# Retention into a bilinear feed-forward on one core: loads and DMA transposes of the last six chunks in another order, two products and a difference moved to GpSimd

## The chip, the cores and the metric

The kernel runs on one core of one Trainium2 chip. The metric is the device time of one execution in microseconds, as the median over the runs of the same program; lower is better. Inside the core, TensorE (PE), VectorE (DVE), ScalarE (ACT), GpSimd (POOL) and SyncE (SP) each work through a list of instructions of their own in a fixed order, and wait for each other through semaphores. In this kernel SP computes nothing: it issues nearly all of the DMAs.

## What is computed

A linear recurrence with one decay rate per head (retention), whose output is the input of a bilinear feed-forward:

```python
def _attn_ref(q, k, v):                       # 4 batches, 8 heads, 768 positions, 64 wide, float32
    gamma = 1.0 - 2.0 ** (-5.0 - np.arange(H))
    scale = 1.0 / np.sqrt(D)
    for t in range(S):
        state = gamma[None, :, None, None] * state + np.einsum('bhd,bhe->bhde', k[:, :, t], v[:, :, t])
        y[:, :, t] = scale * np.einsum('bhd,bhde->bhe', q[:, :, t], state)

x = y.transpose(0, 2, 1, 3).reshape(3072, 512)
out = ((x @ w_a) * (x @ w_b)) @ w_out         # 512 -> 1536 -> 512
```

## The kernel before

**Slots.** The 4 x 768 positions are cut into 24 slots of 128. For a slot the kernel loads k, q and v from HBM (`load_slot`, L117 to L129; q for two slots at once, L138), multiplies k and q with tables of powers of gamma and writes them as bf16 into one tile `kqb` (`scaled`, L281 to L292, two instructions on POOL), casts v to bf16 (`vb`, L251 on POOL, or L249 on ACT for slots 12 to 19), and turns `kqb` into `kqT` with a DMA transpose that SP issues (`flip`, L326 to L329). `casts(t)` (L299) does this for slot t, and between the steps it puts the loads of slot t + 2 on SP's queue.

**PE on a pair of slots.** `turn(new, old)` (L419) takes two slots. For the new pair it updates the running state from `kqb` and `vb` (`update`, matmuls of L375) and computes the scores from `kqT` (`scores`, matmuls of L357, the higher slot of the pair first). For the old pair it computes y (L395 and L405). ACT brings y to SBUF as `xt`, the feed-forward's x.

**Feed-forward.** The slots are joined to blocks (`TILES`, L16): block 4 is slots 10 and 11, block 5 is slots 12 to 15, and the last block is slots 16 to 23. The attention runs ahead of the feed-forward: while PE works on block 5, slots 18 to 23 are loaded, scaled, transposed and scored. Per tile of 128 features a block computes a = x w_a (L553) and g = x w_b (L565); ACT brings a to SBUF (L556), and DVE multiplies it with g from PSUM into h (`ht`, L567). Twelve such tiles make h, and h w_out follows.

**Strassen-Winograd.** The larger products are done with seven block products where eight would be usual, so they need sums of blocks beforehand. `hsum` (L627) makes the sums of h (`hs`), `xf_sum` and `x_sum` those of x, `weight_pieces` those of the weights (`wea`, `web`, `wsa`, `wsb`). In block 5 the class `Quad` (L913) does four of the feature tiles this way: `a` and `b` are its two weights for one pair of tiles, `c` and `d` for the next, and `p1` to `p7` are the seven products (`b5` is product 5 of `b`). Its method `leave` (L954) forms g as product plus snapshot on DVE and then multiplies it with the half of a (`asb`) on DVE or POOL: h = h * asb, SBUF operands only, 128x256 each, all of it at L603, the line of the helper `tt`.

**What sets the order.** All of it is written by hand. The helper `seq` makes each instruction depend on the one before it on the same engine, so that the order of the calls is the order on every engine. The part that the change touches is the string `LACED` (L26), which interleaves the second product of block 4 (`m`) with the Quads of block 5 and with calls such as `S20` (casts of slot 20) or `F2` and `G2` (a and g of feature tile 2), and the calls after it (L1192 to L1207): slots 18 and 19 before the string, 20 and 21 in it, 22 and 23 behind it. SP's queue is one list too: a transpose that stands behind a load is issued after it.

**Names in the rows.** `kf`, `qf`, `vf` are the loaded k, q, v; `kqb` is scaled k and q in natural layout, `kqT` the transposed pair; `ht` is h, `hs1` to `hs4` its sums; `fa`, `fb`, `mA` to `mC`, `uA` to `uC` are PSUM banks of the block products.

Of the kernel before, what the change touches and what calls it, by code (L numbers as in the profile page):

```python
# [12 lines left out]
ALU = mybir.AluOpType  # L13
# [9 lines left out]
       "S02 S01 b7 a2 b2 S04 a6 b6 S13 a5 b5 S12 a3 b3 a4 b4 S11 c7 d7 c6 d6 S14 c5 d5 "  # L23
       "c3 c4 d4 d3")
V_LATE = range(12, 20)
LACED = ("X3 X2 m1 m7 m2 a1 b1 a2 b2 m6 X1 a6 b6 a7 b7 F2 X4 m5 a5 b5 S20 G2 a3 b3 a4 b4 V18 S21 "  # L26
         "m3 c1 d1 F3 H3 c2 d2 c6 d6 c7 d7 c5 d5 m4 c3 d3 V19 c4 d4 G3")
LOADS = "p0 p1 w0 w1 a1 b1 a2 k2 q2 b2 v2 o0 o1 o2 o3 o4 o5 s6 t8".split()

# [2 lines left out]
def kernel(  # L32
# [10 lines left out]
    nc = tc.nc  # L43
    P = 128
    B, H, S, D = q.shape
# [6 lines left out]
    NSLOT = B * NCH  # L52
# [59 lines left out]
    def raw_tile(shape, dtype, tag, name):  # L112
        return raw.tile(shape, dtype, tag=tag, name=name, bufs=3 if tag == "vf" else 2)

    raws, wst, whole = {}, {}, {}

    def load_slot(t, names="kqv"):  # L117
        b, ci = divmod(t, NCH)
        for nm in names:
            src = {"k": k, "q": q, "v": v}[nm]  # L120
            if nm == "q":
                if t % 2 == 0:
                    load_two(nm, src, b, ci // 2, t)
                continue
            if t % 2 == 0:
                whole[nm] = raw_tile([P, 2, H, D], F32, nm + "f", nm + "f")
            raws[nm, t] = whole[nm][:, t % 2]
            s = src[b, :, ci * P : (ci + 1) * P, :].rearrange("h p d -> p h d")
            seq(nc.sync.dma_start(out=raws[nm, t], in_=s))  # L129
# [5 lines left out]
    def load_two(nm, src, b, u, t):  # L135
        f = raw_tile([P, H, 2, D], F32, nm + "f", nm + "f")
        s = src[b, :, 2 * u * P : 2 * (u + 1) * P, :].rearrange("h (p two) d -> p h two d", two=2)
        seq(nc.sync.dma_start(out=f, in_=s))  # L138
        for par in range(2):
            raws[nm, t + par] = f[:, :, par, :]  # L140
# [106 lines left out]
    def cast(engine, dst, src):  # L247
        if engine is nc.scalar:
            seq(nc.scalar.copy(dst, src))  # L249
        else:  # L250
            seq(engine.tensor_copy(dst, src))  # L251
# [19 lines left out]
    kb, qb, vb, kqT, aT = {}, {}, {}, {}, {}  # L271
# [9 lines left out]
    def scaled(eng, t, i):  # L281
        tab = tabs[0] if i else tabs[1 if t < 2 * PAIRS else 2]
        dst, src, tab = kqb[t][:, i], raws["kq"[i], t], tab[:, t % NCH]
        if t < 2 * PAIRS:
            dst, src = (x.rearrange("p (hp r) d -> p hp r d", r=2) if x is src else x
                        for x in (dst, src))
            tab = tab.rearrange("p (hp r) o -> p hp r o", r=2).to_broadcast([P, HP, 2, D])
        else:
            dst = dst.rearrange("p hp r d -> p r hp d")
            src = src.rearrange("p (r hp) d -> p r hp d", r=2)  # L290
            tab = tab.rearrange("p (r hp) o -> p r hp o", r=2).to_broadcast([P, 2, HP, D])
        seq(eng.tensor_tensor(dst, src, tab, op=ALU.mult))  # L292

    def new_nat(t):
        kqb[t] = nat.tile([P, 2, HP, 2, D], BF16, tag="kqb", name="kqb")
        kb[t], qb[t] = kqb[t][:, 0], kqb[t][:, 1]
        vb[t] = nat.tile([P, H, D], BF16, tag="vb", name="vb")

    def casts(t, between=lambda: None):  # L299
        new_nat(t)  # L300
        scaled(nc.gpsimd, t, 0)
        between()
        scaled(nc.gpsimd, t, 1)
        if t not in range(12, 20):
            cast(nc.gpsimd, vb[t], raws["v", t])
        u = t + 2
        if u in (20, 22):
            load_slot(u, "kq")
            load_slot(u + 1, "k")
        flip(t)  # L310
        if u in V_LATE:
            if u == 13:
                load_slot(12, "q")
            elif u == 19:
                load_slot(18, "kq")
            load_slot(u, {12: "k", 18: ""}.get(u, "kq"))
            if u % 2:
                load_slot(u - 1, "v")
                load_slot(u, "v")
        elif u in (20, 22):  # L320
            load_slot(u, "v")
            load_slot(u + 1, "v")
        elif u < 20:
            load_slot(u)

    def flip(t):  # L326
        if t % 2 == 0:
            kqT[t // 2] = tra.tile([P, 2, 2, HP, P], BF16, tag="kqT", name="kqT", bufs=3)
        seq(nc.sync.dma_start_transpose(  # L329
            out=kqT[t // 2][:, t % 2].rearrange("p a b c -> p (a b) c"),  # L330
            in_=kqb[t].rearrange("p a hp r d -> p (a hp r d)")))

    def casts_two(t):
        for u in (t, t + 1):
# [267 lines left out]
    def tt(dst, x, y, op, eng=nc.vector):  # L602
        seq(eng.tensor_tensor(dst, x, y, op=op))  # L603
# [23 lines left out]
    def hsum(J, s, a, b, eng=nc.vector):  # L627
        U = slice(int(J == 0), 2 if isinstance(J, tuple) else TILES[J] // 2)
        hs_tile(J, s)
        v = ht[J].rearrange("p (k j) (u r n) -> p r k j u n", k=2, r=2, n=P)  # L630
        A11, A12, A21, A22 = (v[:, r, k2, a:b, U] for r in range(2) for k2 in range(2))
        S = {x: hs[J, x][:, a:b, U] for x in (1, 2, 3, 4) if (J, x) in hs}
        x, y, op = {3: (A11, A21, ALU.subtract), 2: (A22, S[3], ALU.subtract), 1: (A21, A22, ALU.add),
                    4: (A12, S.get(2), ALU.subtract)}[s]
        tt(S[s], x, y, op, eng)
# [116 lines left out]
    def laced(order):  # L752
        made = {"m": Group(4, 0, Y0, AT0, Y1)}
        for p in range(2):
            made.update({"ac"[p]: Quad(p, "a", AT1, "kqT2"), "bd"[p]: Quad(p, "b", Y1, "aT")})
        ht[5] = htp.tile([P, NFT, 4 * P], BF16, tag="ht", name="ht")
        for x in order.split():
            if x[0] == "H":
                hsum(5, int(x[1]), 0, 1)
            elif x[0] in "XFGVS":  # L760
                {"X": xf_sum, "F": lambda f: (store(), ffn_a(5, f)), "G": lambda f: ffn_g(5, f), "V": v_cast,
                 "S": casts}[x[0]](int(x[1:]))
            else:
                getattr(made[x[0]], "p" + x[1])()

# [147 lines left out]
    class Quad:  # L913
# [40 lines left out]
        def leave(self, i, c, bank, n):  # L954
            cols = slice(c * DH, (c + 1) * DH)
            if self.w == "a":
                tt(self.half(i)[:, cols], self.bank[bank], self.snaps[n], ALU.add)
                return
            h = ht[5][:, NP * i + self.p, cols]
            tt(h, self.bank[bank], self.snaps[n], ALU.add)  # L960
            tt(h, h, self.half(i)[:, cols], ALU.mult, nc.gpsimd if (i, c) == (1, 0) else nc.vector)

        def p1(self):
            self.A = self.whole(FF)
# [64 lines left out]
    D_, G_, A_ = nc.vector, nc.gpsimd, nc.scalar  # L1029
    K, Q = 0, 1  # L1030
# [167 lines left out]
    hsums(4, 3, 6, G_)  # L1198
    casts(19)
    laced(LACED)  # L1200
    casts(22)
    turn(18, 16)
    hsum(5, 3, 1, 2)
    hsum(5, 2, 0, 2, G_)
    casts(23)
    blocks(5, 4, 6)
    blocks(5, 8, 9)  # L1207
    weight_pieces(2)
# [37 lines left out]
```

## Time and profile before

| | us |
|---|---|
| runs shown | 219.98, 220.09, 223.73 |
| median | 220.09 |
| the profiled execution: its time | 220.76 |
| its span in the profile | 219.0 |
| PE busy | 210.7 (96% of the span) |
| POOL busy | 153.5 (70%) |
| DVE busy | 149.8 (68%) |
| ACT busy | 102.9 (47%) |
| granted TensorE clock, mean | 0.998 |

The time of the profiled execution is 1.76 us more than its span, since the span begins at the first instruction and ends at the last. A busy PE means that its matmuls follow one another; their ends are modelled. The page's DMA share is that of the mean of 16 DMA engines and goes above 1 where transfers overlap in the records. Rows of the timeline give the start, the duration, the engine, the line and the tiles, and in brackets how long the engine stood idle just before and who ended it.

### The profile page before, as it was taken

The page shows a single profiled execution, that of the slowest core. Times are in us where ns is not written, and L with a number is a line of the kernel's source. Part 1 is how long each engine was busy: PE and PEld are TensorE (multiplying, and loading weights), DVE is VectorE, ACT ScalarE, POOL GpSimd, SP SyncE. Part 2 cuts the span into 40 slices and gives each one's busy share as a digit, 9 for nine tenths or more (in the row PEclk, how much of TensorE's full clock was granted, in tenths as well). Part 3 has the DMA queues.
Part 4 walks back from the last instruction along what each step waited for, and adds up shares of the span by engine and source line. Part 5 has one row for each costly group of instructions (what it writes and reads, how often), then busy time and mean ns, then how long its engine had stood idle before and what let it go on. Part 6 is the DMA issues. An engine that isn't in the chain of part 4 may idle for free.

```text
span 219.0 us, 5716 instructions
## 1 busy us (share of the span) xinstructions
PE 210.7 (96%) x2252; PEld 146.0 (67%) x2252; DVE 149.8 (68%) x276; ACT 102.9 (47%) x231; POOL 153.5 (70%) x184
## 2 busy tenths in 40 slices
PE   7889999999999999999999999799999999999994
PEld 3557445687458888888888776356874444448883
DVE  3777346846984494464478989477576987788962
ACT  3256325342234435464566566344546566652331
POOL 5266876778778759989679968599996999540000
PEclk9999999999999999999999999999999999999999
DMA  6999999999999999999998999950013000000055
GB/s 167 290 322 367 385 308 359 381 253 234 200 257 239 203 230 221 188 221 264 166 229 208 217 189 217 221 122 3 3 48 145 0 0 3 1 0 0 27 192 168
DMA packets 85162, 39.68 MB, mean 181 GB/s; under 512 B 57488, under 2 KB 78864, under 8 KB 85136
## 3 DMA queue, kind: packets, MB, share of 16 engines
q1 hardware_dynamic: 84992, 39.26, 77.3%
q8 instruction: 17, 0.28, 0.5%
q14 instruction: 9, 0.07, 0.1%
q10 hardware_dynamic: 144, 0.07, 0.1%
HBM read 28.31 MB, written 6.29 MB: 158 GB/s over the span
## 4 chain that ended last, share of the span: by engine, by line
PE 82%; DMA 6%; DVE 4%; SPq 3%; POOL 1%; issue 1%; DVEq 0%
PE a L553 16%; PE g L565 16%; PE mA L670 11%; PE uA L844 9%; PE mB L670 6%; PE o L590 5%; PE uB L844 5%; SPq L138 3%; DMA wsta<-in_moe_w_a_dram 3%; PE mC L670 3%; DMA kqT<-kqb 3%; PE uC L844 2%; PE at L357 2%; PE y L405 2%; DVE ht L603 1%; PE st L375 1%
## 5 line engine op out<-in xcount | busy, mean ns | idle before, releaser
L567 DVE TENSOR_TENSOR ht<-g,asb 128x256 bf16<-128x256 f32 (+1 forms) x70 | 34.4, 492 | 30.8 <-PE g L565 27.8
L553 PE MATMUL a<-xt,wa_bf 128*128 128x256 bf16 (+1 forms) x280 | 48.6, 300 | 0.1
L565 PE MATMUL g<-xt,wb_bf 128*128 128x256 bf16 (+1 forms) x280 | 48.4, 300 | 0.0
L556 ACT CAST asb<-a 128x256 bf16<-128x256 f32 (+1 forms) x70 | 30.0, 428 | 34.6 <-PE a L553 32.9
L565 PEld LDWEIGHTS <-wb_bf 128*128 128x128 bf16 x280 | 27.0, 98 | 10.2
L553 PEld LDWEIGHTS <-wa_bf 128*128 128x128 bf16 x280 | 26.5, 98 | 10.7 <-POOL wa_bf L251 0.4
L292 POOL TENSOR_TENSOR kqb<-kf,ktab 128x512 bf16<-128x512 f32 x22 | 23.3, 1064 | 6.8 <-DMA kf<-in_k_dram 4.6
L851 ACT COPY snap<-uA 128x512 f32<-128x512 f32 x36 | 20.0, 587 | 15.4 <-PE uA L844 13.9
L670 PEld LDWEIGHTS <-hs 128*128 128x128 bf16 x234 | 22.8, 98 | 3.6
L363 DVE TENSOR_TENSOR aT<-at,mask 128x512 bf16<-128x512 f32 x36 | 22.3, 681 | 1.9 <-PE at L357 1.7
L292 POOL TENSOR_TENSOR kqb<-qf,qtab 128x512 bf16<-128x512 f32 x18 | 19.3, 1070 | 4.0 <-DMA qf<-in_q_dram 4.0
L603 POOL TENSOR_TENSOR ht<-gsb,asb 128x512 bf16<-128x512 bf16 x13 | 15.2, 1174 | 7.2 <-DVE gsb L603 7.1
L677 ACT COPY snaps<-mA 128x256 f32<-128x256 f32 x30 | 11.0, 374 | 19.0 <-PE mA L670 18.9
L670 PEld LDWEIGHTS <-ht 128*128 128x128 bf16 x180 | 17.5, 98 | 3.3
L251 POOL CAST vb<-vf 128x512 bf16<-128x512 f32 x16 | 9.9, 635 | 11.4 <-DMA vf<-in_v_dram 9.5
L603 POOL TENSOR_TENSOR hs<-ht 128x384 bf16<-128x384 bf16 (+2 forms) x13 | 15.2, 1167 | 3.0 <-DVE ht L567 3.0
L603 POOL TENSOR_TENSOR hs<-ht,hs 128x384 bf16<-128x384 bf16 (+1 forms) x17 | 16.8, 993 | 0.6 <-DVE ht L567 0.5
L670 PE MATMUL mA<-wsum,hs 128*128 128x256 bf16 x120 | 15.2, 273 | 0.0
L603 DVE TENSOR_TENSOR osb<-mB,snaps 128x256 f32<-128x256 f32 x20 | 8.4, 421 | 8.6 <-ACT snaps L677 4.7
L590 PE MATMUL o<-wo_bf,ht 128*128 128x512 bf16 x48 | 10.7, 379 | 0.0
L249 ACT CAST gst<-st 128x256 bf16<-128x256 f32 x14 | 5.2, 372 | 11.3 <-PE st L375 11.3
L603 DVE TENSOR_TENSOR gsb<-uB,snap 128x512 bf16<-128x512 f32 x12 | 8.2, 686 | 2.9 <-ACT snap L851 2.1
(138 smaller groups left out, 375.9 us busy)
## 6 DMA issues: line engine op xcount, KB each, us to landing
qf<-in_q_dram SPq DMA_DIRECT2D x12, 512.0 KB, 6.1
out_dram<-osb SPq DMA_DIRECT2D x21, 256.0 KB, 4.0
kf<-in_k_dram SPq DMA_DIRECT2D x18, 256.0 KB, 5.4
vf<-in_v_dram SPq DMA_DIRECT2D x18, 256.0 KB, 5.3
wsta<-in_moe_w_a_dram SPq DMA_DIRECT2D x6, 512.0 KB, 7.7
wsto<-in_moe_w_out_dram SPq DMA_DIRECT2D x6, 512.0 KB, 8.7
wstb<-in_moe_w_b_dram SPq DMA_DIRECT2D x5, 512.0 KB, 8.2
kf<-in_k_dram SPq DMA_DIRECT2D x3, 512.0 KB, 7.2
```

The lines of the kernel that those rows point to most:

```text
L292: seq(eng.tensor_tensor(dst, src, tab, op=ALU.mult))
L363: seq(nc.vector.tensor_tensor(aT[t][:, r], at[r], mask.to_broadcast([P, HP, P]), op=ALU.mult))
L553: seq(nc.tensor.matmul(a, wa_bf[:, kt, fs], xcols(J, kt, c0, c1), start=(kt == 0), stop=(kt == KT - 1)))
L556: seq(nc.scalar.copy(asb, a))
L565: seq(nc.tensor.matmul(g, wb_bf[:, kt, fs], xcols(J, kt, c0, c1), start=(kt == 0), stop=(kt == KT - 1)))
L567: seq(nc.vector.tensor_tensor(ht[J][:, ft, c0:c1], g, asbs.pop((J, ft, c0)), op=ALU.mult))
L590: seq(nc.tensor.matmul(o, ht[J][:, ft, i * P : (i + 1) * P], wo_bf[:, ft], start=(ft == 0), stop=(ft == NFT - 1), skip_group_check=True))
L603: seq(eng.tensor_tensor(dst, x, y, op=op))
L670: seq(nc.tensor.matmul(m, w, right[:, j], start=(first and j == 0), stop=(j == NP - 1), skip_group_check=True))
L677: seq(nc.scalar.copy(self.snaps[:, n], self.bank["A"]))
L844: seq(nc.tensor.matmul(m, w, right[:, k], start=(first and k == 0), stop=(k == 1), skip_group_check=True))
L851: seq(nc.scalar.copy(self.snaps[n], self.bank["A"]))
```

## The change

The change rewrites the order around slots 18 to 23:

- `casts(18)` no longer puts all loads of slots 20 and 21 between its scaling and its transpose. SP now issues the k and q loads of slot 20, the transpose of 18, the k load of 21; then, with `casts(19)`, the transpose of 19, both v loads, and the k and q loads of slot 22.
- Slots 20 and 21 are scaled together (`late_kq`, as K20), all four scalings and both transposes one behind the other; the k load of 23 and the v loads of 22 and 23 come behind the transposes. The casts of v of both slots follow as `late_v` (L20), later in the string. Slots 22 and 23 are done in the same manner behind the string, ahead of and behind `turn(18, 16)`.
- In `Quad.leave` POOL makes all products h * asb with i = 1, where before it made one of two. In block 5 that moves two products (b5 and d5) from DVE to POOL; a 128x256 difference, `hsum(5, 3, 1, 2)`, moves as well. Two differences of h stand ahead of the scaling of slots 22 and 23.

```diff
-LACED = ("X3 X2 m1 m7 m2 a1 b1 a2 b2 m6 X1 a6 b6 a7 b7 F2 X4 m5 a5 b5 S20 G2 a3 b3 a4 b4 V18 S21 "
+LACED = ("X3 X2 m1 m7 m2 a1 b1 a2 b2 m6 X1 a6 b6 a7 b7 F2 X4 m5 a5 b5 K20 G2 a3 b3 a4 b4 V18 L20 "
          "m3 c1 d1 F3 H3 c2 d2 c6 d6 c7 d7 c5 d5 m4 c3 d3 V19 c4 d4 G3")
...
 def casts(t, between=lambda: None):
...
         u = t + 2
-        if u in (20, 22):
+        if u == 20:
             load_slot(u, "kq")
+        flip(t)
+        if u == 20:
             load_slot(u + 1, "k")
-        flip(t)
+            return
+        if u == 21:
+            load_slot(u - 1, "v")
+            load_slot(u, "v")
+            load_slot(22, "kq")
+            return
...
-        elif u in (20, 22):
-            load_slot(u, "v")
-            load_slot(u + 1, "v")
...
+    def late_kq(t):
+        for u in (t, t + 1):
+            new_nat(u)
+            scaled(nc.gpsimd, u, 0)
+            scaled(nc.gpsimd, u, 1)
+            flip(u)
+        if t == 20:
+            load_slot(23, "k")
+            load_slot(22, "v")
+            load_slot(23, "v")
+
+    def late_v(t):
+        for u in (t, t + 1):
+            cast(nc.gpsimd, vb[u], raws["v", u])
...
-            tt(h, h, self.half(i)[:, cols], ALU.mult, nc.gpsimd if (i, c) == (1, 0) else nc.vector)
+            tt(h, h, self.half(i)[:, cols], ALU.mult, nc.vector if i == 0 else nc.gpsimd)
...
     laced(LACED)
-    casts(22)
+    hsum(5, 3, 1, 2, G_)
+    hsum(5, 2, 0, 2, G_)
+    late_kq(22)
     turn(18, 16)
-    hsum(5, 3, 1, 2)
-    hsum(5, 2, 0, 2, G_)
-    casts(23)
+    late_v(22)
```

**SP, from the first load of slot 20 to the transpose of slot 21.** `kqb_2288` is slot 18; slots 19, 20 and 21 are `kqb_2432`, `kqb_2534` and `kqb_2569` before, and `kqb_2429`, `kqb_2538` and `kqb_2544` now. `kf_2292` is k of slots 20 and 21; the next `kf` is k of 22 and 23. Before:

```order
L129 DMA kf_2292<-in_k_dram 128x8x64
L138 DMA qf_2294<-in_q_dram 128x8x128
L129 DMA kf_2292<-in_k_dram 128x8x64
L329 DMA_TRANSPOSE kqT_2297<-kqb_2288 128x8x128
L129 DMA vf_2299<-in_v_dram 128x8x64 x2
L329 DMA_TRANSPOSE kqT_2297<-kqb_2432 128x8x128
L129 DMA kf_2539<-in_k_dram 128x8x64
L138 DMA qf_2541<-in_q_dram 128x8x128
L129 DMA kf_2539<-in_k_dram 128x8x64
L329 DMA_TRANSPOSE kqT_2544<-kqb_2534 128x8x128
L129 DMA vf_2546<-in_v_dram 128x8x64 x2
L329 DMA_TRANSPOSE kqT_2544<-kqb_2569 128x8x128
```

On the same queue in the changed kernel:

```order
L129 DMA kf_2292<-in_k_dram 128x8x64
L138 DMA qf_2294<-in_q_dram 128x8x128
L333 DMA_TRANSPOSE kqT_2296<-kqb_2288 128x8x128
L129 DMA kf_2292<-in_k_dram 128x8x64
L333 DMA_TRANSPOSE kqT_2296<-kqb_2429 128x8x128
L129 DMA vf_2434<-in_v_dram 128x8x64 x2
L129 DMA kf_2437<-in_k_dram 128x8x64
L138 DMA qf_2439<-in_q_dram 128x8x128
L333 DMA_TRANSPOSE kqT_2542<-kqb_2538 128x8x128
L333 DMA_TRANSPOSE kqT_2542<-kqb_2544 128x8x128
L129 DMA kf_2437<-in_k_dram 128x8x64
L129 DMA vf_2550<-in_v_dram 128x8x64 x2
```

The transposes of slots 20 and 21 (the last two transposes of each list) moved ahead of the second k load and both v loads of slots 22 and 23; in the first half each transpose moved ahead of loads too.

**POOL, from the scaling of slot 20 to the sum `hs2`.** `asb_2527` and `asb_2627` before, `asb_2531` and `asb_2627` now, are the halves of a with which the Quads multiply h. Before:

```order
L292 TENSOR_TENSOR kqb_2534<-kf_2292,ktab1_175 128x2x4x64
L292 TENSOR_TENSOR kqb_2534<-qf_2294,qtab_146 128x2x4x64
L251 CAST vb_2535<-vf_2299 128x512
L603 TENSOR_TENSOR ht_2437<-ht_2437,asb_2527 128x256
L292 TENSOR_TENSOR kqb_2569<-kf_2292,ktab1_175 128x2x4x64
L292 TENSOR_TENSOR kqb_2569<-qf_2294,qtab_146 128x2x4x64
L251 CAST vb_2570<-vf_2299 128x512
L603 TENSOR_TENSOR ht_2437<-ht_2437,asb_2627 128x256
L292 TENSOR_TENSOR kqb_2661<-kf_2539,ktab1_175 128x2x4x64
L292 TENSOR_TENSOR kqb_2661<-qf_2541,qtab_146 128x2x4x64
L251 CAST vb_2662<-vf_2546 128x512
L603 TENSOR_TENSOR hs2_2767<-ht_2437,hs3_2601 128x512
```

On POOL in the changed kernel:

```order
L622 TENSOR_TENSOR ht_2441<-ht_2441,asb_2531 128x256
L292 TENSOR_TENSOR kqb_2538<-kf_2292,ktab1_175 128x2x4x64
L292 TENSOR_TENSOR kqb_2538<-qf_2294,qtab_146 128x2x4x64
L292 TENSOR_TENSOR kqb_2544<-kf_2292,ktab1_175 128x2x4x64
L292 TENSOR_TENSOR kqb_2544<-qf_2294,qtab_146 128x2x4x64
L622 TENSOR_TENSOR ht_2441<-ht_2441,asb_2531 128x256
L251 CAST vb_2539<-vf_2434 128x512
L251 CAST vb_2545<-vf_2434 128x512
L622 TENSOR_TENSOR ht_2441<-ht_2441,asb_2627 128x256 x2
L622 TENSOR_TENSOR hs3_2601<-ht_2441 128x256
L622 TENSOR_TENSOR hs2_2662<-ht_2441,hs3_2601 128x512
```

The product b5 now stands ahead of the scaling of slot 20, and the scaling of slots 22 and 23 (behind these rows, k and q of 22, k and q of 23, then both casts of v) stands behind both sums and behind two casts of v.

**DVE, around the product b5.** `fb` and `fa` are PSUM banks of the Quads, `g` that of feature tile 2. Before:

```order
L603 TENSOR_TENSOR ht_2437<-fb_2504,snapf_2475 128x256
L603 TENSOR_TENSOR ht_2437<-ht_2437,asb_2527 128x256
L567 TENSOR_TENSOR ht_2437<-g_2549,asb_2512 128x512
L603 TENSOR_TENSOR ht_2437<-fb_2471,asb_2482 128x256
L603 TENSOR_TENSOR asb_2527<-fa_2501,snapf_2469 128x256
```

On DVE in the changed kernel:

```order
L622 TENSOR_TENSOR ht_2441<-fb_2508,snapf_2479 128x256
L586 TENSOR_TENSOR ht_2441<-g_2553,asb_2516 128x512
L622 TENSOR_TENSOR ht_2441<-fb_2475,asb_2486 128x256
L622 TENSOR_TENSOR asb_2531<-fa_2505,snapf_2473 128x256
L622 TENSOR_TENSOR ht_2441<-fb_2508,snapf_2478 128x256
```

The product of `ht` with `asb` between the sum from `fb` and the product from `g` has left DVE.

More of the change, by code (lines that the diff above doesn't have):

```diff
@@ L319, in casts @@
                 load_slot(u, "v")
-        elif u in (20, 22):
-            load_slot(u, "v")
-            load_slot(u + 1, "v")
-        elif u < 20:
+        elif u < NSLOT:
             load_slot(u)
@@ L759, in laced @@
                 hsum(5, int(x[1]), 0, 1)
-            elif x[0] in "XFGVS":
+            elif x[0] in "XFGVKL":
                 {"X": xf_sum, "F": lambda f: (store(), ffn_a(5, f)), "G": lambda f: ffn_g(5, f), "V": v_cast,
-                 "S": casts}[x[0]](int(x[1:]))
+                 "K": late_kq, "L": late_v}[x[0]](int(x[1:]))
             else:
```

## The prediction

> **What bounds the kernel now.** I read the page's busy times first, then the waits of the stretch that the change touches, then PE's timeline there, and last the queues of SP, POOL and DVE that feed it. First the page's busy times of two engines:
>
> ```profile
> PE 210.7 (96%) x2252; PEld 146.0 (67%) x2252; DVE 149.8 (68%) x276; ACT 102.9 (47%) x231; POOL 153.5 (70%) x184
> ```
>
> PE is busy 210.7 of 219.0 us, so no rearrangement can win more than PE's idle time, and what lies at the start and the end is not touched. What is left is in the waits between 110 and 180 us and in PE's timeline:
>
> ```profile
> PE at L357 <- DMA kqT<-kqb: 1.7, 1, 1.7
> ...
> PE fa L934 <- DVE ht L567: 0.5, 1, 0.5
> ```
>
> ```profile
> 126.77 0.82 PE L670 MATMUL mA<-wo_bf,hs 128*128 128x256 bf16 x6
> 128.08 0.38 PE L934 MATMUL fa<-xt,wa_bf 128*128 128x256 bf16 x2 [0.49 <-DVE ht L567]
> ...
> 140.65 0.32 PE L375 MATMUL st<-vb,kqb 128*64 128x64 bf16 x8
> 142.72 0.64 PE L357 MATMUL at<-kqT 64*64 64x128 bf16 x32 [1.75 <-DMA kqT<-kqb]
> ...
> 149.38 0.64 PE L357 MATMUL at<-kqT 64*64 64x128 bf16 x32
> ...
> 153.12 0.82 PE L670 MATMUL mA<-wsum,hs 128*128 128x256 bf16 x6
> ```
>
> PE stands still twice: 0.49 us until DVE's product of feature tile 2 frees a bank, and 1.75 us in `turn(20, 18)` until the transpose of slot 21 has landed (the higher slot is scored first). Together 2.24 us: that is all that the change can win here. Next the queue that issues those transposes, SP's timeline:
>
> ```profile
> 119.65 2.91 SPq L129 DMA_DIRECT2D kf<-in_k_dram  x1
> 122.67 2.60 SPq L329 DMA_TRANSPOSE kqT<-kqb  x1
> 125.37 1.15 SPq L129 DMA_DIRECT2D vf<-in_v_dram  x2
> 126.62 2.08 SPq L329 DMA_TRANSPOSE kqT<-kqb  x1
> 128.75 0.65 SPq L129 DMA_DIRECT2D kf<-in_k_dram  x1
> 129.45 0.70 SPq L138 DMA_DIRECT2D qf<-in_q_dram  x1
> 130.19 1.81 SPq L129 DMA_DIRECT2D kf<-in_k_dram  x1
> 132.11 3.11 SPq L329 DMA_TRANSPOSE kqT<-kqb  x1
> 135.32 1.15 SPq L129 DMA_DIRECT2D vf<-in_v_dram  x2
> 136.57 2.39 SPq L329 DMA_TRANSPOSE kqT<-kqb  x1
> ```
>
> From 119.65 to 138.96 each issue begins about 0.1 us or less behind the end of the one before, so SP's place in line decides, not its waits. The last row is the transpose of slot 21. Its inputs were ready much earlier, as POOL's timeline shows:
>
> ```profile
> 118.85 1.04 POOL L292 TENSOR_TENSOR kqb<-qf,qtab 128x512 bf16<-128x512 f32 x1
> ...
> 123.87 1.22 POOL L292 TENSOR_TENSOR kqb<-qf,qtab 128x512 bf16<-128x512 f32 x1
> ...
> 129.81 0.67 POOL L603 TENSOR_TENSOR ht<-ht,asb 128x256 bf16<-128x256 bf16 x1
> 130.43 1.05 POOL L292 TENSOR_TENSOR kqb<-kf,ktab 128x512 bf16<-128x512 f32 x1
> 131.43 1.09 POOL L292 TENSOR_TENSOR kqb<-qf,qtab 128x512 bf16<-128x512 f32 x1
> ...
> 139.36 0.61 POOL L251 CAST vb<-vf 128x512 bf16<-128x512 f32 x1 [2.61 <-DMA vf<-in_v_dram]
> 139.93 1.15 POOL L603 TENSOR_TENSOR hs<-ht,hs 128x512 bf16<-128x512 bf16 x1
> ...
> 143.03 0.61 POOL L251 CAST vb<-vf 128x512 bf16<-128x512 f32 x1
> ...
> 149.48 2.26 POOL L603 TENSOR_TENSOR hs<-ht,hs 128x512 bf16<-128x512 bf16 x2
> ```
>
> The rows at 118.85, 123.87 and 131.43 are q of slots 18, 19 and 21: slot 21 was scaled by 132.52, and its transpose left at 136.57, 4.05 us later. The DMA engines have no slack meanwhile. This is the row of the stretch 119.6 to 142.7 (its last two columns are the DMA share and GB/s), and the time to landing of seven issues (the last number of a row), in this order: transpose of slot 21, transpose of slot 20, k of slot 23, v of 22 (right behind a transpose), v of 23, q of slots 20 and 21 (the longest of this stretch), transpose of slot 23 (when the loads are through):
>
> ```profile
> 119.60:142.70 23.10, 20.87 (x220) 14.23 (x217) 18.69 (x38) 12.01 (x30) 17.59 (x20) 1.00 1.19 207
> ```
>
> ```profile
> kqT<-kqb SPq DMA_TRANSPOSE x1, 6.1
> ...
> kqT<-kqb SPq DMA_TRANSPOSE x1, 5.5
> ...
> kf<-in_k_dram SPq DMA_DIRECT2D x1, 256.0 KB, 6.5
> ...
> vf<-in_v_dram SPq DMA_DIRECT2D x1, 256.0 KB, 3.9
> ...
> vf<-in_v_dram SPq DMA_DIRECT2D x1, 256.0 KB, 4.3
> ...
> qf<-in_q_dram SPq DMA_DIRECT2D x1, 512.0 KB, 6.9
> ...
> kqT<-kqb SPq DMA_TRANSPOSE x1, 3.1
> ```
>
> So the engines are saturated at 207 GB/s (share 1.19), and a transfer lands 3.9 to 6.9 us after its issue while the queue is full, 3.1 us when it is not. The first wait is on DVE:
>
> ```profile
> 125.97 0.41 DVE L603 TENSOR_TENSOR ht<-fb,snapf 128x256 bf16<-128x256 f32 x1
> 126.41 1.02 DVE L603 TENSOR_TENSOR ht<-ht,asb 128x256 bf16<-128x256 bf16 x1
> 127.35 0.68 DVE L567 TENSOR_TENSOR ht<-g,asb 128x512 bf16<-128x512 f32 x1
> ```
>
> **The change, part by part.**
>
> *Product b5 leaves DVE.* The 1.02 us row goes. The product with g then starts at 126.41, ends at 127.09, and PE's `m3` ends at 127.59 (126.77 + 0.82): the bank is free 0.5 us before PE asks. PE's wait of 0.49 us goes, and everything on PE behind it comes 0.49 us earlier. d5 and the difference leave DVE at a place where no PE wait is put down to DVE: worth nothing there, hidden behind PE's matmuls.
>
> *POOL takes them over.* Two products at 0.67 us (the row at 129.81 is the same form), and one difference of 128x256 that POOL has not done before: not less than nothing, not more than the 1.15 us of the 128x512 row, and nearest to the 0.67 of the equally large product. Sum 2.0 us. b5 must wait for DVE's row at 125.97, so it runs from 126.4 to 127.1, while POOL now starts slot 20 at 125.09. That puts q of slot 20 at 129.2 and q of slot 21 at 131.2 (four scalings of 1.05, no cast between). The 2.61 us that POOL waited for v at 139.36 covers the 2.0 us.
>
> *The transposes on SP.* The transpose of 18 must wait for q of slot 18 (119.89) and starts 0.25 us after SP is free; it and the k load of 21 then take what they took before (2.91 + 2.60), to 125.4. Transpose of 19: its q is ready at 125.09, so no wait; 2.08, to 127.5. Both v: 1.15; k and q of 22: 0.65 + 0.70; that makes 130.2 with the gaps. Transpose of 20 (q at 129.2, no wait) 3.11, and that of 21 leaves at 133.4 where it left at 136.57. With 5.5 to 6.1 us it lands at 138.9 to 139.5. A second way: it has passed one k and two v loads, 3 x 262 KB, which at 207 GB/s are 3.8 us, so 142.67 - 3.8 = 138.9. PE wants it at 140.97 - 0.49 = 140.48. The 1.75 us go, with 1.0 us or more to spare.
>
> Here the Trainium skill speaks against the change. Its page "DMA: Bandwidth & Descriptors", section "Specifications", puts the HBM limit of a core at about 358 GB/s; by an estimate from that figure the three loads are 2.2 us and the transpose would land at 140.5, with nothing to spare. The same section says that transfers under 512 B do not reach line rate, and k and v have rows of 64 float32, 256 B; the measured 207 GB/s agrees with that, and I keep it.
>
> *What is passed comes later.* The second k of 22 and 23 left at 130.19 and landed at 136.7. It now stands behind two transposes (2 x 262 KB, 2.5 us): 139.2 by bytes; by issue it leaves at 133.4 + 2.39 = 135.8 and lands 3.9 us (the v right behind a transpose) to 6.5 us later, 139.7 to 142.3. I take 140.2, near the lower end, since its like is a load behind transposes (3.9 and 4.3), with a little for the second transpose ahead of it. POOL is ready for it: v of 20 and 21 until about 133, d5, d4, the two sums until 136.1, k and q of 22 until 138.2. So k of 23 starts at 140.2, q ends at 142.2, and both casts of v end at 143.4, where the cast at 143.03 ended at 143.64 before. Two things hang on that. The transpose of 23 leaves at 142.3 and lands at 145.4; PE wants it at 149.42 - 2.24 = 147.2: hidden, 1.8 us to spare. And POOL's later sums: the second of the two at 149.48 is the last part of `hs2`, done at 151.7, which is 8.1 us after the last cast of v. PE's matmuls with `hs2` begin at 153.12, and the fifth of its six is the first that needs this part, about 0.5 us later (four sixths of 0.82): slack 1.9 us, and the 2.24 us won eat it. Now it is done at 143.4 + 8.1 = 151.5, and PE wants it at 153.6 - 2.24 = 151.4: a new wait of 0.1 us. Each us by which the k load lands later than 140.1 is a us of that wait; at 139.2 there is none, at 142.3 it is 2.2.
>
> Everything behind that follows PE: the weight sums on POOL have us to spare, and DVE and ACT wait for PE there.
>
> Sum: 0.49 + 1.75 - 0.1 = 2.14 us. Against the profiled execution's own 220.76 that is 218.6; this execution lies 0.67 above the median of the runs shown, 220.09, and from that it is 217.95, so 218.0.
>
> **The rivals.**
>
> *POOL becomes the bound at `hs2`.* The k load of slot 23 lands at 140.6 to 141.8, since it stands behind two transposes in a saturated queue; PE then waits 0.5 to 1.7 us at 151.4. For it: 6.5 us is what the same load took before. Against it: the v loads behind a transpose took 3.9 and 4.3. Time: 218.4 to 219.6.
>
> *No change.* The two transposes back to back might slow each other, so that the second still lands after 142. Then only the 0.49 us are left, or a late k load gives all back: 219.6 to 220.3. Against it: none of the transposes of this stretch took more than 6.1 us, and it would need 8.7.
>
> *Slower.* The k load of 23 lands so late that the transpose of 23 stops PE in `turn(22, 20)`. Landing L, then two scalings (2.0), issue (0.1) and 3.1: PE goes on at L + 5.2 where it would have at 147.2, and `hs2` is at L + 11.3. It decides from L = 142.3, where the 2.2 us of wait at `hs2` are what was won. At L = 144 the time would be 221.8; at 146.8 it would be 224.6, over 2%. Nothing among the loads here took more than 6.9 us, and that needs 8 to 11 (issue at 135.8).
>
> **How the numbers follow.** The forecast, 217.6 to 218.4, gets 0.60; POOL as the bound 0.23; no change 0.08; slower 0.09, of which 0.03 is over 2%. Range 217.5 to 219.7: from all of the 2.24 us and a little spread of the runs to the end of the first rival, 0.83 in all. 2% is 4.4 us, about what a measurement of this kernel can tell from no change; PE's idle time caps the gain at half of that, so faster by over 2% gets 0.01, slower 0.03, within 0.96.
>
> **What would show it.** In the changed profile PE waits neither for DVE's product with g near 127.6 nor for `kqT` near 140.5; SP's two transposes stand side by side and the second leaves near 133.4; the second k load lands near 140.2; POOL's wait for `vf` is replaced by one for `kf`; PE may show a short wait for `hs` near 151. I am wrong if `kqT` still ends a wait of PE, or if PE waits over 0.6 us for `hs`, or if a wait on `vb` or `kqb` that is not there now appears in a `turn`.

## The result and the profile after

| | before | after |
|---|---|---|
| median of the runs, us | 220.16 (11 runs, 219.07 to 223.73) | 218.51 (11 runs, 218.44 to 219.61) |
| the profiled execution: time, span | 220.76, 219.0 | 218.49, 216.8 |
| mean granted clock there | 0.998 | 1.000 |

The ratio of after to before is 0.9935, 95% interval 0.9906 to 0.9964: some 0.65% faster, which is within 2%. The ratios, here and below, leave out runs more than 1.5% above the fastest of their kernel (for before those of 222 us and more), the medians contain them, and so the ratio of a kernel with many slow runs rests on the few that the table names. The two profiled spans differ by 2.2 us.

The page's busy times after. PE's work is the same as before within 0.3 us, its share is higher, and POOL has 1.9 us more of it (155.4 against 153.5):

```profile
PE 210.4 (97%) x2240; PEld 146.4 (68%) x2252; DVE 149.2 (69%) x273; ACT 102.8 (47%) x231; POOL 155.4 (72%) x187
```

The view of PE's waits between 110 and 180 us has no line left. PE's timeline at the two places that had a wait, and at the sums of h:

```profile
126.77 0.82 PE L689 MATMUL mA<-wo_bf,hs 128*128 128x256 bf16 x6
127.42 0.38 PE L953 MATMUL fa<-xt,wa_bf 128*128 128x256 bf16 x2
...
140.24 0.32 PE L394 MATMUL st<-vb,kqb 128*64 128x64 bf16 x8
140.48 0.64 PE L376 MATMUL at<-kqT 64*64 64x128 bf16 x32
...
147.14 0.64 PE L376 MATMUL at<-kqT 64*64 64x128 bf16 x32
...
150.89 0.82 PE L689 MATMUL mA<-wsum,hs 128*128 128x256 bf16 x6
```

The scores of slot 21 begin at 140.48 where they began at 142.72, with no bracket behind the row. The matmuls with `hs2` run through in 0.82 us: PE does not wait for `hs2` either. On DVE the product with g now stands right behind the sum of `fb` and the snapshot, at 126.30 instead of 127.35:

```profile
125.97 0.41 DVE L622 TENSOR_TENSOR ht<-fb,snapf 128x256 bf16<-128x256 f32 x1
126.30 0.67 DVE L586 TENSOR_TENSOR ht<-g,asb 128x512 bf16<-128x512 f32 x1
```

SP's timeline: the transposes of slots 20 and 21 stand side by side, and both are issued by 134.70, where slot 21's alone was issued from 136.57 to 138.96. The first two rows are the k load of slot 21 and the transpose of slot 19:

```profile
122.90 0.58 SPq L129 DMA_DIRECT2D kf<-in_k_dram  x1
125.13 1.23 SPq L333 DMA_TRANSPOSE kqT<-kqb  x1
...
128.64 0.89 SPq L138 DMA_DIRECT2D qf<-in_q_dram  x1
129.64 5.06 SPq L333 DMA_TRANSPOSE kqT<-kqb  x2
134.76 0.57 SPq L129 DMA_DIRECT2D kf<-in_k_dram  x1
135.42 1.72 SPq L129 DMA_DIRECT2D vf<-in_v_dram  x2
137.24 0.82 SPq L598 DMA_DIRECT2D out_dram<-osb  x1
138.17 3.84 SPq L333 DMA_TRANSPOSE kqT<-kqb  x2
```

Taken one by one, the row at 129.64 is 3.35 us for slot 20 and, from 133.09, 1.62 us for slot 21. Slot 21's transpose landed 3.6 us after 133.09, at 136.7, where before it took 6.1 us from 136.57, to 142.67.

And POOL's timeline, from the difference that it had not done before (0.67 us) over the wait for k of slot 23 to the last part of `hs2`:

```profile
134.19 0.67 POOL L622 TENSOR_TENSOR hs<-ht 128x256 bf16<-128x256 bf16 x1
...
138.46 1.04 POOL L292 TENSOR_TENSOR kqb<-kf,ktab 128x512 bf16<-128x512 f32 x1 [0.37 <-DMA kf<-in_k_dram]
...
140.45 1.17 POOL L251 CAST vb<-vf 128x512 bf16<-128x512 f32 x2
...
147.58 2.27 POOL L622 TENSOR_TENSOR hs<-ht,hs 128x512 bf16<-128x512 bf16 x2
```

k of slot 23 landed at 138.4, 3.7 us after its issue at 134.76; `hs2` was complete at 149.85, and PE needs its last part four sixths into the row at 150.89, at about 151.4. So 1.5 us of slack are left there. The DMA engines moved a little more in the same stretch (1.12, 217 GB/s, against 1.19, 207):

```profile
119.60:142.70 23.10, 22.89 (x284) 15.81 (x286) 19.67 (x38) 13.10 (x33) 21.30 (x26) 1.00 1.12 217
```

### The profile page after: what moved, and what is told of

Same layout as the page of the kernel before. It is cut to its first block, busy times and chain, and to the rows that moved or that the text cites. A ratio compares the mean times of both kernels' runs of the same rounds, so it can differ in the third digit from the quotient of the medians.

```text
span 216.8 us, 5705 instructions
## 1 busy us (share of the span) xinstructions
PE 210.4 (97%) x2240; PEld 146.4 (68%) x2252; DVE 149.2 (69%) x273; ACT 102.8 (47%) x231; POOL 155.4 (72%) x187
## 4 chain that ended last, share of the span: by engine, by line
PE 89%; SPq 3%; DMA 3%; DVE 1%; issue 1%; ACT 1%; POOL 0%; ACTq 0%
PE a L572 18%; PE g L584 18%; PE mA L689 12%; PE uA L863 9%; PE mB L689 6%; PE o L609 5%; PE uB L863 4%; SPq L138 3%; DMA wsta<-in_moe_w_a_dram 3%; PE mC L689 3%; PE at L376 2%; PE uC L863 2%; PE y L424 2%; PE st L394 2%; PE fa L953 2%; PE fb L953 1%
## 5 line engine op out<-in xcount | busy, mean ns | idle before, releaser
L622 POOL TENSOR_TENSOR hs<-ht 128x384 bf16<-128x384 bf16 (+3 forms) x14 | 15.8, 1132 | 2.1 <-DVE ht L586 2.1
L622 DVE TENSOR_TENSOR asb<-uB,snap 128x512 bf16<-128x512 f32 x12 | 8.2, 685 | 2.9 <-ACT snap L870 2.0
```

## The experiments

The theory is the prediction's: two waits of PE are gone, 0.49 us by the products on POOL and 1.75 us by the place of slot 21's transpose on SP; what was passed (the loads of k of 23 and of v) has slack behind it. The rivals are that one of the two parts carries all, that the joint scaling and not the order of the loads matters, and that POOL at `hs2` or slot 23's transpose is close to the bound. The experiments ran in three sets, A, B and C, each beside runs of before of its own, with medians of 219.97, 220.37 and 219.19 us; set C ran on another chip than A and B. In the table, "0.992" counts the runs with that mean clock (or 0.990 for one of them); all other runs had 0.997 to 1.000.

| kernel | set | median us (range, runs) | 0.992 | ratio to before of its set, 95% interval |
|---|---|---|---|---|
| before | A | 219.97 (218.89 to 223.16, 35) | 5 | 1 |
| the change without its products on POOL | A | 218.94 (218.83 to 219.30, 12) | 0 | 0.9957 [0.9935, 0.9979] |
| the products alone | A | 221.82 (218.33 to 223.40, 12) | 8 | 0.9962 [0.9915, 1.0010], of 4 runs |
| the loads behind slot 21's transpose alone | A | 219.63 (219.07 to 221.01, 12) | 0 | 1.0004 [0.9974, 1.0034] |
| the change, slots 20 and 21 scaled apart | B | 218.50 (218.06 to 219.44, 12) | 0 | 0.9932 [0.9904, 0.9960] |
| the change, no slots scaled jointly | C | 218.85 (218.34 to 219.53, 12) | 0 | 0.9983 [0.9963, 1.0003] |
| the change, k of 23 between the transposes | B | 218.50 (218.47 to 218.88, 12) | 0 | 0.9947 [0.9924, 0.9970] |
| the change, k of 23 behind v of 22 and 23 | A | 221.00 (219.53 to 223.50, 12) | 4 | 1.0050 [1.0011, 1.0090], of 10 runs, 2 of them at 0.992 |
| before, slot 21's transpose behind slot 22's | B | 223.80 (221.77 to 224.48, 4) | 3 | 1.0167 [1.0115, 1.0219], of 4 runs, 3 of them at 0.992 |

The median of before differs between the sets, since its runs fall in three groups of varying size; so ratios of different sets are compared with care. No experiment moves the two sums ahead of slot 22 alone, or the loads around the transposes of slots 18 and 19 alone.

**The change without its products on POOL.**

```diff
-            tt(h, h, self.half(i)[:, cols], ALU.mult, nc.vector if i == 0 else nc.gpsimd)
+            tt(h, h, self.half(i)[:, cols], ALU.mult, nc.gpsimd if (i, c) == (1, 0) else nc.vector)
```

> The changed kernel with the products b5 and d5 back on DVE; order of loads, transposes and sums as changed. If the 0.49 us that PE waited for DVE is a term of its own and on the path: that wait is back near 127.6 us, no wait for kqT, about 218.9 to 219.0 us, 0.4 to 0.5 over the changed kernel. Rival (the product's place is hidden by later slack, the transposes carry the whole gain): as the changed kernel, 218.5 us.

PE's waits between 110 and 180 us have this one line:

```profile
PE fa L953 <- DVE ht L586: 0.5, 1, 0.5
```

The wait on DVE is back, alone, and the median is 0.43 us above that of the change. So, in the change, the products are worth about the 0.49 us that the prediction gave them.

**The products alone.**

```diff
-            tt(h, h, self.half(i)[:, cols], ALU.mult, nc.gpsimd if (i, c) == (1, 0) else nc.vector)
+            tt(h, h, self.half(i)[:, cols], ALU.mult, nc.vector if i == 0 else nc.gpsimd)
```

> The kernel before with only the products with i = 1 moved to GpSimd. If the two waits lie in a chain: PE's 0.49 us near 127.6 go, the transpose of slot 21 lands when it did, so PE's wait for kqT grows by as much (about 2.2 us), and the time stays that of before within 0.2 us. Rival (the two gains add up, each by itself): 0.5 us faster than before.

Four runs took 218.33 to 220.04 us, eight took 221.66 to 223.40 at a clock of 0.992. The median, 221.82, meets neither forecast: the theory had the time of before, the rival 0.5 us less. The profiled execution is the fastest of the twelve, and PE waits nowhere in it. SP's row of slot 21's transpose, which begins at 135.49 where the profile before has 136.57:

```profile
135.49 2.00 SPq L329 DMA_TRANSPOSE kqT<-kqb  x1
```

It landed 4.2 us after that, at 139.7, and PE reads it at 140.31. The DMA engines moved more from 130 to 140 us in this execution; the row of that stretch, first of this kernel, then of before:

```profile
130.00:140.00 10.00, 9.89 (x127) 5.91 (x126) 7.73 (x17) 5.37 (x13) 8.39 (x11) 1.00 1.17 227
```

```profile
130.00:140.00 10.00, 10.00 (x132) 6.33 (x131) 8.75 (x19) 5.41 (x14) 6.45 (x9) 1.00 1.30 208
```

The ten microseconds ahead show the same (230 GB/s against 209), and SP was 0.9 us ahead already at the transpose of slot 19. Why this execution moved more is not known. The same program thus has runs without the wait and, by their times, runs with a long one: if the eight lost 1.7 us to the clock, as is worked out below, their spans of 219.9 to 221.7 leave 1.6 to 3.4 us of wait over the 216.6 of this trace. That is an estimate; no trace shows one of the eight. What is shown: alone, this half of the change brings eight of twelve runs to 0.992, where before has five of 35. That PE then comes to the scores earlier and the transpose does not is the likely reason, and is argued.

**The loads behind slot 21's transpose alone.** Loads of k of slot 23 and v of slots 22 and 23 go behind slot 21's transpose, all else as before.

```diff
         if u in (20, 22):
             load_slot(u, "kq")
+        if u == 20:
             load_slot(u + 1, "k")
         flip(t)
+        if u == 23:
+            load_slot(u, "k")
+            load_slot(u - 1, "v")
+            load_slot(u, "v")
...
-        elif u in (20, 22):
+        elif u == 20:
```

> The kernel before with only the k load of 23 and the v loads of 22 and 23 put behind the transpose of 21; POOL's and DVE's order as before. If the place in SP's queue is what held that transpose: it leaves near 133.3 and lands by 139.5, no wait of PE for kqT, 0.49 us near 127.6 stay; v of 22 lands about 0.5 us later ahead of POOL's work, hs2 is done near 152.2 and PE waits about 0.3 us for it; 219.0 to 219.3 us. Rival (POOL's scaling order is what makes the transpose early): the wait for kqT stays over 1 us, time as before.

PE's waits, and the longest DMA wait of POOL's:

```profile
PE mA L675 <- POOL hs L608: 1.3, 1, 1.3
PE fa L939 <- DVE ht L572: 0.5, 1, 0.5
```

```profile
POOL vb L251 <- DMA vf<-in_v_dram: 6.2, 2, 3.6
```

The wait for `kqT` is gone in this execution, and none of the twelve runs is at 0.992. So the place on SP's queue is what held slot 21's transpose, and in this trace the loads around the transposes of slots 18 and 19, which are as before, need not move for it. But 1.3 us are given back at `hs2`, where 0.3 were forecast: the order on POOL is still that of before, the cast of v of slot 22 stands ahead of a sum of h and of slot 23's scaling, and begins at 141.03 where it began at 139.36. This execution is one of the slower of its kernel (220.77); five of the twelve took 219.07 to 219.25, which leaves little beside the 0.49 us, and the median is 219.63. Moving the loads takes the wait away; that the gain stays in most runs needs more of the change. Which part is not shown one by one: the experiments below bear on the joint scalings and the casts of v, none on the sums ahead of slot 22.

**Slots 20 and 21 apart, in the change.** The loads and slots 22 and 23 stay as in the change.

```diff
-LACED = ("X3 X2 m1 m7 m2 a1 b1 a2 b2 m6 X1 a6 b6 a7 b7 F2 X4 m5 a5 b5 K20 G2 a3 b3 a4 b4 V18 L20 "
+LACED = ("X3 X2 m1 m7 m2 a1 b1 a2 b2 m6 X1 a6 b6 a7 b7 F2 X4 m5 a5 b5 S20 G2 a3 b3 a4 b4 V18 S21 "
...
+    def late_one(t):
+        new_nat(t)
+        scaled(nc.gpsimd, t, 0)
+        scaled(nc.gpsimd, t, 1)
+        flip(t)
+        if t == 21:
+            load_slot(23, "k")
+            load_slot(22, "v")
+            load_slot(23, "v")
+        cast(nc.gpsimd, vb[t], raws["v", t])
```

> The changed kernel, with slots 20 and 21 scaled apart again, as before (k and q of 20 in the place of the joint step, k and q of 21 in the place of the two casts of v), the loads and the order of slots 22 and 23 as in the change. Theory (the gain of the transfers' part is that loads of k of 23 and v of 22 and 23 no longer stand ahead of slot 21's transfer on SP; that the scaling of two slots is joined is worth nothing for 20 and 21): slot 21's scaling ends some 3 us later than after, slot 21's transfer leaves SP at about 136 to 137 as in the profile before or earlier, so the wait is between none and 1 us, time 218.4 to 219.2, and above all no run with the clock at 0.992. Rival (the joint scaling is what brings slot 21 early): TensorE waits 1.5 to 2 us for kqT of slot 21 as before, time 219.9 to 220.6, some runs at 222 or above.

The median is that of the change (218.50 and 218.51). SP's row of slots 20 and 21:

```profile
129.73 5.28 SPq L333 DMA_TRANSPOSE kqT<-kqb  x2
```

It begins 0.1 us and ends 0.3 us later than that of the change, although slot 21's scaling ended 2.2 us later on POOL (133.38 against 131.18). The theory was right on the time, and too cautious on the transpose, which I had put at 136 to 137. Joining the scaling of slots 20 and 21 is worth no time that these runs show: the order of the loads does it. It is worth slack at `hs2`. POOL's row of its last part, then PE's row that reads it:

```profile
148.79 2.27 POOL L629 TENSOR_TENSOR hs<-ht,hs 128x512 bf16<-128x512 bf16 x2
```

```profile
150.68 0.82 PE L696 MATMUL mA<-wsum,hs 128*128 128x256 bf16 x6
```

`hs2` is complete at 151.06, 1.2 us later than in the change, and PE needs it at about 151.2.

**No slots scaled jointly.** As the kernel before this one, and slots 22 and 23 apart too.

```diff
-    late_kq(22)
+    late_one(22)
     turn(18, 16)
-    late_v(22)
+    late_one(23)
```

> The changed kernel with no scaling of two slots joined: slots 20 and 21 apart as in the experiment before, and slots 22 and 23 apart too, so that GpSimd casts v of slot 22 ahead of the scaling of k and q of slot 23. What stays of the change are the order of the loads on SP, the sums of ht into hs ahead of slot 22, and the products on GpSimd. Theory (for slots 22 and 23 the joint scaling is needed): in the profile after, k of 23 is scaled from 138.5 to 140.5 with its transfer leaving SP by 142, and TensorE starts its last scores on the transposes at 147.1; the cast of slot 22's v (two at 1.17 us each pair, 0.6 us) must now wait for v's landing at about 140.5 to 141.5, so slot 23's transfer leaves SP 2 to 3.5 us later, at 144 to 145.5 with a landing of 3 to 4 us, and TensorE waits 0.5 to 2 us for kqT of slot 23: time 219.0 to 220.5, some runs with the clock at 0.992 and above 221. Rival (joining the scalings is worth nothing anywhere, the order of the loads alone carries the gain): no wait of TensorE, 218.4 to 218.7 like the change.

The theory was wrong in its wait: PE does not wait for the transpose of slot 23, and the view of its waits between 110 and 180 us has no line. The profiled execution is again the fastest of its twelve (218.34), but its `hs2` is late enough to be touched: POOL's row, then PE's.

```profile
148.84 2.27 POOL L629 TENSOR_TENSOR hs<-ht,hs 128x512 bf16<-128x512 bf16 x2
```

```profile
150.63 0.93 PE L696 MATMUL mA<-wsum,hs 128*128 128x256 bf16 x6
```

`hs2` is complete at 151.11, 1.26 us later than in the change, and the six matmuls take 0.93 us in place of 0.82. Nearly all of that lateness is in the trace of the experiment before this one too (151.06), so it comes with taking slots 20 and 21 apart; taking 22 and 23 apart as well adds 0.05 us in these two traces. The twelve runs spread from 218.34 to 219.53, and their median is 0.34 us above that of the change. But this is set C, whose before was faster too, and the interval of the ratio to it contains 1. So whether the joint scaling of slots 22 and 23 is worth any time stays open. No trace shows one of the longer runs.

**k of slot 23 between the transposes.**

```diff
             flip(u)
+            if u == 20:
+                load_slot(23, "k")
         if t == 20:
-            load_slot(23, "k")
             load_slot(22, "v")
```

> The changed kernel, with the load of k of slot 23 issued between the transposing transfers of slots 20 and 21 instead of behind both. Slot 21's transfer then leaves SP 0.5 to 1.5 us later than at 138.2 of the profile after, against scores that TensorE starts at 140.5 and reads for slot 21 some 3 us later. Theory (what set the time before was the landing of slot 21's transfer, and after it there is slack of some microseconds): no wait for slot 21, the 0.37 us wait of GpSimd for k of slot 23 gone, which was hidden anyway, time 218.3 to 218.7, ratio to the kernel after 1.000. Rival (the order of after is tight, each microsecond of the queue counts): a wait for kqT of 0.5 to 1.5 us at the scores in most runs, 219.0 to 220.0, and some runs with the clock at 0.992 and 221 or more.

No wait of PE, POOL's for `kf` is gone, and 218.50, as the theory had it. The 138.2 in the expectation was a misreading: that row of the profile after is the transposes of slots 22 and 23. Slot 21's began at 133.09 there, and it is the one that PE reads first, at 140.48. SP's row of slot 21's transpose here:

```profile
134.47 1.75 SPq L333 DMA_TRANSPOSE kqT<-kqb  x1
```

It is 1.4 us later than in the change and still in time. So there is room on this side of the order of the change; the next kernel tries the other. The range, 0.4 us, is the narrowest of all, but twelve runs against eleven don't show it to be better than the change.

**k of slot 23 behind v of slots 22 and 23.**

```diff
         if t == 20:
-            load_slot(23, "k")
             load_slot(22, "v")
             load_slot(23, "v")
+            load_slot(23, "k")
```

> The changed kernel with the k load of 23 behind both v loads of 22 and 23. Two loads ahead are about 2.4 us: k lands near 140.8, POOL's wait for it grows from 0.37 to about 2.7 us, hs2 is done near 152.2 where PE wants it at 151.4, so PE waits about 0.8 us for hs2: 219.3 us. If POOL's slack at hs2 is larger than reckoned: 218.5 us, no wait of PE. If the transpose of 23 is the first to be late: a wait of PE for kqT near 147 us.

POOL's and PE's longest waits in the profiled execution, which took 223.35 us:

```profile
POOL kqb L292 <- DMA kf<-in_k_dram: 3.3, 1, 3.3
```

```profile
PE mA L689 <- POOL hs L622: 1.9, 1, 1.9
PE at L376 <- DMA kqT<-kqb: 1.0, 1, 1.0
```

Both places that the prediction's rivals named are there, and at the times of its formulas. k of 23 landed at L = 143.1, not near 140.8 as was expected of this kernel; the transpose was to release PE at L + 5.2 = 148.3, and `hs2` to be done at L + 11.3 = 154.4. POOL's two rows:

```profile
143.09 1.04 POOL L292 TENSOR_TENSOR kqb<-kf,ktab 128x512 bf16<-128x512 f32 x1 [3.33 <-DMA kf<-in_k_dram]
```

```profile
152.22 2.25 POOL L622 TENSOR_TENSOR hs<-ht,hs 128x512 bf16<-128x512 bf16 x2
```

Not all of the 4.7 us that k came later than in the change is the two loads: in this execution SP was through with the transposes of slots 20 and 21 only at 136.10, 1.4 us later than in the change, and their order is the same. PE's timeline:

```profile
148.25 0.64 PE L376 MATMUL at<-kqT 64*64 64x128 bf16 x32 [0.96 <-DMA kqT<-kqb]
...
154.53 0.39 PE L689 MATMUL mA<-wsum,hs 128*128 128x256 bf16 x2 [1.93 <-POOL hs L622]
...
155.76 1.38 PE L689 MATMUL mB<-wsum,hs 128*128 128x256 bf16 x6
```

The two waits are 2.9 us, but the span is 4.8 us longer than that of the change. The last row shows the rest: six matmuls that take 0.82 us elsewhere take 1.38. The windows around it (the number before the last two is the granted clock):

```profile
155.00:156.00 1.00, 1.00 (x34) 0.80 (x27) 0.00 (x0) 0.56 (x2) 1.00 (x2) 0.94 0.00 0
156.00:157.00 1.00, 1.00 (x7) 0.69 (x6) 0.13 (x1) 0.84 (x2) 1.00 (x2) 0.50 0.00 0
157.00:158.00 1.00, 1.00 (x6) 0.70 (x5) 0.91 (x2) 0.00 (x0) 0.92 (x2) 0.50 0.00 0
158.00:159.00 1.00, 1.00 (x7) 0.74 (x5) 0.94 (x1) 0.37 (x1) 1.00 (x2) 0.50 0.00 0
159.00:160.00 1.00, 1.00 (x10) 0.81 (x9) 0.00 (x0) 0.37 (x1) 1.00 (x2) 0.85 0.08 16
```

If the clock is either 1 or one half, it was halved for 0.12 + 3 + 0.30 = 3.4 us, which is 1.7 us of work lost. With the 2.9 us of waits that is 4.6 of the 4.8 us. Whether such a drop follows a long wait is what the last experiment asks.

**Slot 21's transpose behind slot 22's, in before.**

```diff
-        flip(t)
+        if t != 21:
+            flip(t)
+        if t == 22:
+            flip(21)
```

> The kernel before, with slot 21's transposing transfer issued behind slot 22's, some 5 us later than it was, so that it must land late in every run. In the profile before, TensorE waits 1.75 us for it. Theory (a stall of TensorE near 2 us or above also takes the granted clock to one half for about 3.4 us, as the trace of the experiment with k of slot 23 behind v of 22 and 23 shows): TensorE waits 4 to 6 us at the scores, the rows of a microsecond behind it show a granted clock of 0.50 for 3 us or more, mean clock 0.992 or below, time 223.5 to 226.5 in all runs, no run at 219 or 221. Rival (the clock has nothing to do with the stall, and the runs at 223 us of the kernel before are an accident of the chip): clock 1.0 in most runs, and a time that grows by the added wait alone, 222.5 to 224.5, spread over the same three groups as the kernel before.

PE's timeline in the profiled execution (224.18 us, span 222.4), with the same product before and behind the wait:

```profile
139.04 1.03 PE L556 MATMUL a<-xt,wa_bf 128*128 128x512 bf16 x4
...
144.52 0.64 PE L360 MATMUL at<-kqT 64*64 64x128 bf16 x32 [3.35 <-DMA kqT<-kqb]
...
146.08 1.89 PE L556 MATMUL a<-xt,wa_bf 128*128 128x512 bf16 x4
147.76 1.67 PE L568 MATMUL g<-xt,wb_bf 128*128 128x512 bf16 x4
149.27 1.03 PE L556 MATMUL a<-xt,wa_bf 128*128 128x512 bf16 x4
```

And its windows there:

```profile
145.00:146.00 1.00, 1.00 (x44) 0.81 (x33) 1.00 (x2) 0.40 (x2) 1.00 (x2) 0.82 1.13 305
146.00:147.00 1.00, 1.00 (x7) 0.37 (x4) 1.00 (x3) 1.00 (x2) 1.00 (x2) 0.50 0.17 64
147.00:148.00 1.00, 1.00 (x4) 0.36 (x3) 0.47 (x1) 0.05 (x1) 0.92 (x2) 0.50 0.00 0
148.00:149.00 1.00, 1.00 (x3) 0.30 (x2) 0.00 (x0) 0.58 (x1) 0.28 (x1) 0.50 0.00 0
149.00:150.00 1.00, 1.00 (x6) 0.48 (x5) 0.46 (x1) 0.00 (x0) 0.00 (x0) 0.97 0.00 0
```

Over the 216.8 of the change this span has 5.6 us: 3.35 of this wait, 0.51 of the one on DVE, and 1.7 of half clock (0.36 + 3 + 0.06 = 3.4 us of it). The wait was 3.35 us, not the 4 to 6 expected, and the time 224.18 lies in the range of both forecasts; what tells them apart is the clock. Three of four runs are at 0.992, and the half clock stands right behind the wait, so the rival, that the clock has nothing to do with the wait, does not fit. But one of the four runs took 221.77 at a clock of 1.000, which I had not expected: its span of 220.0 leaves, as an estimate, 2.7 us for this wait beside the 0.5, and the clock held. So the length of a wait does not decide alone.

## Why the prediction was right, and which of its terms was mis-sized

**What bounds the kernel.** Right: PE's idle time capped the gain. The two waits named were all that PE had between 110 and 180 us, and the span is shorter by their sum, 2.2 us.

**The product b5.** Right, 0.49 forecast and 0.43 measured by taking it out again (medians of different sets of runs). The difference whose form was not in the trace before took POOL 0.67 us, the value taken.

**The transposes on SP.** Right in place and sign: slot 21's began at 133.09 where 133.4 was forecast, and PE reads it at 140.48 without a wait. But two terms on the way were wrong, and it was luck that the start came out. The k load of slot 21 was given the 2.91 us that it took before; it took 0.58, and SP then stood idle until 125.13, when POOL had scaled slot 19, where the forecast was 125.4 with no wait. And the landing was forecast for 138.9 to 139.5, from the 5.5 to 6.1 us and the 207 GB/s of before; it came at 136.7, 3.6 us after the start. So PE had 3.8 us to spare, not 1.0, and 207 GB/s was no ceiling. The experiments add that the joint scaling has no part in the start for slots 20 and 21. The Trainium skill's 358 GB/s (page "DMA: Bandwidth & Descriptors", section "Specifications") was not reached over this stretch after the change either: 217 GB/s.

**k of slot 23.** The mechanism was right, its time was not: 138.4 where 140.2 was forecast. SP issued it at 134.76, not 135.8, and it landed in 3.7 us, below the 3.9 that I had taken as the lower end. So the 0.1 us of wait at `hs2` did not come, and 1.5 us of slack stayed. The two formulas behind it hold: from L = 138.4 `hs2` is due at 149.7 and was done at 149.85, and with k put behind v both times were met to 0.1 us.

**The sum.** Against the profiled execution it gave 220.76 - 2.14 = 218.6, and that is the change's 218.5. Taken from the median it gave 217.95, so 218.0, and that was 0.5 us too low. The time after, 218.51, is thus 0.1 us outside the forecast's 217.6 to 218.4, and inside the interval of the first rival, whose wait at `hs2` did not come. The mis-sized term is the 1.75 us: they are the wait of one execution, not of the median one. The median of the runs shown lies 0.67 us lower, and on the same floor it can then have no more than 2.24 - 0.67 = 1.57 us of waits to give back: 220.09 - 1.57 = 218.5. The floor is common (216.7 to 216.9 us of span in eight of the eleven runs after; single runs of other kernels here have 216.3 to 216.6), and the change brings most runs to it. So before's runs are best read as floor plus wait, which is an estimate from their spans: of its 35 runs in set A 17 have spans of 217.1 to 217.6, the 0.49 us wait and little more; 13 have 218.3 to 219.3, a wait for `kqT` of about 1 to 2 us as in the trace; 5 have 221.2 to 221.4 at a clock of 0.992, which fits a wait of some 2.3 us and the 1.7 of half clock that two traces of other kernels show. That last assignment is argued, since no trace of such a run of before exists.

**The rivals.** POOL at `hs2`: not in the change, but 1.5 us away. PE waited there when k of 23 came 4.7 us later (1.93 us) and when the loads alone were moved (1.3 us). No change: it needed 8.7 us from the start of slot 21's transpose to its landing, and that took 3.6. Slower: not the change, but the kernel with k of slot 23 behind two loads of v, 0.5% over before, interval 0.1% to 0.9%. Its waits came at the forecast's formulas; the forecast's price for that case left out the clock.

## What to carry to other kernels

A wait for a transfer in a full queue can vary by microseconds from run to run, as it does here by the spans. So a gain that consists of it is subtracted from the execution that showed it, or better: the time after is the floor (span less waits of the bounding engine), whatever the median was. Of two changes that each take away a wait, the upstream one alone can be worthless or harmful: here the products alone had eight of twelve runs at 0.992. When a load is put behind others on a queue, look at the work that stands behind it on its consumer: here the loads alone took one wait away and gave back 1.3 us at `hs2` in the trace, behind a cast that waited for v.

## What the runs showed of the hardware

A stall of PE can cost more than its length. In two traces waits of 1.93 us (with one of 0.96 us that had ended 4.4 us before it began) and 3.35 us were followed, 1.1 to 1.4 us after PE had gone on, by a granted clock of 0.50 for 3.4 us, and that took 1.7 us more. In the trace before, with a wait of 1.75 us, the clock was 1.00 in each microsecond from 143 to 149, and it held in one run with some 2.7 us of wait by its span. The Trainium skill, page "TensorE: Matmul & The Clock Gate", section "What's actually happening", says that the clock is halved after at least one idle window of about 3.4 us, that full speed comes back after at least one busy window of about the same length, and that the window runs free of the kernel. The 3.4 us at half clock agree, and a free-running window would explain why the length does not decide alone; that a whole window must be idle does not agree, since both waits are shorter than 3.4 us, the one of 1.93 us clearly. No run here measured where the window lies.

The same loads and transposes on SP moved 208 GB/s from 130 to 140 us in the trace of before and 227 in that of the products alone. Slot 21's transpose landed 6.1 us after the start of its issue before, 4.2 with the products alone and 3.6 in the change. Issues on SP vary too: in the profile after, the transposes of slots 20 and 21 took 3.35 and 1.62 us to issue, and those of slots 22 and 23 1.48 and 1.47.
